# Gated mix of linear attention and a ReLU layer: the first x block evacuated from two banks, all x transposes ahead of the first slab, the gate row behind two later units

## The chip, the cores and the metric

The kernel runs on one core of a Trainium2 chip. The metric is the device time of one execution, in microseconds (us). A core has five engines with a queue each: TensorE (PE: matmuls; its weight loads are listed apart as PEld), VectorE (DVE), ScalarE (ACT), GpSimd (POOL) and SyncE (SP), which here issues nearly all DMA transfers. They run side by side and wait for one another by semaphores. Matmuls write to PSUM, an accumulator of 128 partitions with 8 banks of 512 fp32 columns; VectorE and ScalarE carry results from there to SBUF ("evacuation").

## The reference

```python
x = A_x                                             # [1, 2048, 512] bf16
g = sigmoid((x * gate_w).sum(-1, keepdims=True))    # one gate per row
a = A(x, wqkv, w_phi, wo)                           # linear attention, 32 heads of 16
b = relu(x @ w1) @ w2                               # w1 [512, 1376], w2 [1376, 512]
out = g * a + (1 - g) * b
# A: q, k, v = heads of x @ wqkv;  pq = q @ w_phi, pk = k @ w_phi (per head)
#    phi = concat(softmax(p), softmax(-p));  kv = phi_k^T v,  z = sum phi_k
#    a = concat_heads(phi_q @ kv / (phi_q . z + 1e-6)) @ wo
```

The branch b uses the same x as a. What the change touches is the start of the first matmul of b, x @ w1, and the gate's product x · gate_w.

## The kernel before

**How the work is written.** `_Plan` (L14) holds one list of instructions per engine, in the order in which the Python code calls `p.op` and `p.dma`. Each engine runs its list in that order. An instruction names the events that it waits for (`after`) and the one that it sets (`ev`); events become semaphore counts. There is no scheduler: the order is the one written out. `free[bank]` is a table that is kept while the lists are written: the event after which a PSUM bank may be written again, set by whoever plans the last evacuation of that bank.

**Transposed x.** Matmuls need x with d on the partitions, as XT (4 d tiles of 128, 2048 rows). Rows 0 to 511 (the first "chunk" of four) come as they are, by two loads of 256 rows each (`loadx0`, halves 0 and 1, j = 0, 1 and 2, 3), and are transposed on TensorE by 16 matmuls of 128 columns against the identity IDN (`xtr`, L235), evacuated to XT by VectorE or ScalarE (`xev`, L247). The three other chunks are transposed by DMA (L189) and come much later.

**The start on TensorE**, in its order (L537 to L562): five warm-up matmuls of ones, 512 columns each; the gate row (`gatecol(3)`, L223: the four 128-blocks of gate_w, loaded to GR, are turned by one matmul with 4 output columns in bank 3, and VectorE copies them into column DFF of W1); a sixth warm-up of 384 columns; then the transposes. Called a and b by half, they are: a0 (half 0, d tiles 0 and 1: four blocks, bank 6), the first two blocks of a1 (half 0, d tiles 2 and 3, bank 7), which are all from the first load; then b0 (half 1, d tile 0: two blocks, bank 2), the rest of a1, b1 (half 1, d tiles 1 and 2: four blocks, bank 1). VectorE evacuates a0 in two instructions, ScalarE b0, a1 and b1, in this order. Two transposes are left, b2 (half 1, d tile 3), which use bank 2 again after b0.

**Slabs.** The first eight of the ten units of 128 columns of x @ w1 are not computed unit by unit but by d tile: `slab(t)` (L529) issues, for each of eight units, the matmul of d tile t into the unit's own bank, so that the first slab needs only the first piece of W1. The order of banks is UB = (3, 4, 5, 0, 6, 7, 2, 1). The first slab is cut: four units, then the transposes b2, evacuated by VectorE, then four units; the seventh unit writes bank 2, and so waits for b2's evacuation. `XA` and `XB` name the evacuations that the four slabs wait for. VectorE sets a few tiles to constants (L553 to L560), and eight ReLUs (`relu`, L264) evacuate the units to HT, ScalarE and VectorE in turn.

**Units and banks.** All later units are made by `hunit` (L279: four accumulating matmuls of 512 columns, then a ReLU). They and `rest` (L289, the last 96 columns of w1 with the gate column beside them, for a chunk) and V tile 1 take their bank from `nextbank()` (L275), a counter that gives 3, 4, 5 in turn. Units 8 and 9 of chunk 0 follow the slabs, then V tiles 0 and 1, the products of w_phi and wqkv (`pre`), V tile 2 and `rest(0)`, which is the first to read the gate column.

**The two phases.** The main loop (L586) goes over 16 row tiles: q and k scores (`atile`, banks 0 and 1), V (`vtile`, bank 2), the accumulation of kv (`kv`, banks 6 and 7), and in between units of chunks 1 to 3 by the lists `mid` and `late` (the last six: (3, 4) to (3, 9)). The second phase (L614 to L638) is the output: `nd(m)` (L464: attention output of a row tile, banks 0 and 1 or 2 and 3 by turns), `finB` (L489: relu(x @ w1) @ w2, 11 matmuls), `finA` (L500: attention @ wo) and `comb` (L512: mixes the two and stores). Its banks are written out by hand: `finB(0, 4)` at L617, and (4, 5, 7) in turn for later tiles. All of them wait for `free[bank]`. It begins with

```python
nd(0)
qchain(NT - 1)
gate()
finB(0, 4)
nd(1)
```

With the counter as it stands, the last three units (3, 7), (3, 8), (3, 9) have banks 4, 5 and 3.

Of the kernel before, what the change touches and what calls it, by code (L numbers as in the profile page):

```python
# [5 lines left out]
ACT = mybir.ActivationFunctionType  # L6
# [62 lines left out]
def bass_gated_mix__linear_kernel_hedgehog__dense_activation_relu__prompt_kernel(  # L69
# [17 lines left out]
    P = 128  # L87
# [17 lines left out]
    with ExitStack() as es:  # L105
        E = es.enter_context
        XT = E(nc.sbuf_tensor("XT", [P, NDT, S], BF16))
# [18 lines left out]
        IDN = E(nc.sbuf_tensor("IDN", [P, P], BF16))  # L126
# [14 lines left out]
        PS = E(nc.psum_tensor("PS", [P, 8, 512], FP32))  # L141

        XS = OT[:, 0, :].rearrange("p (j d) -> p j d", j=4)
# [7 lines left out]
        p = _Plan(["sp", "pool", "act", "dve", "pe"])  # L151
        free = {b: [] for b in range(8)}
# [24 lines left out]
        for t in range(1, NDT):  # L177
            loadw1(t, 0, 8 * P)
        p.dma("sp", lambda e: e.dma_start(
            out=W1[:, :, 8 * P:DFF], in_=B_w1[:, 8 * P:DFF].rearrange("(j p) n -> p j n", p=P)), "w1r", ev="w1r")  # L180
        p.dma("sp", lambda e: e.dma_start(
            out=WPS[:, :, :], in_=A_w_phi.rearrange("(g hl) r c -> (hl r) g c", g=NDT)), "wps", ev="wps")
        p.dma("sp", lambda e: e.dma_start(
            out=WV[:, :, :], in_=A_wqkv[:, 2 * D:3 * D].rearrange("(j p) n -> p j n", p=P)), "wv", ev="wv")
        for i in range(2):
            p.dma("sp", lambda e, i=i: e.dma_start_transpose(
                out=WQKT[:, 4 * i:4 * i + 4, :], in_=A_wqkv[:, i * D:(i + 1) * D]), f"wqk{i}", ev=f"wqk{i}")
        for c in range(1, NCH):
            p.dma("sp", lambda e, c=c: e.dma_start_transpose(  # L189
                out=XT[:, :, c * 512:(c + 1) * 512], in_=x2[c * 512:(c + 1) * 512, :]), f"x{c}", ev=f"x{c}")  # L190
# [9 lines left out]
            after=["wps"], ev="wd")  # L200
        for gt in range(NDT):
# [4 lines left out]
                after=["wd", "m8"], ev=f"wbd{gt}")  # L206
# [5 lines left out]
             after=["iota0"], ev="idn")  # L212
        p.op("dve", lambda e: e.tensor_single_scalar(ROW8[:, :], ROW8[:, :], 4, ALU.arith_shift_right),
             after=["iota"], ev="r8")
# [3 lines left out]
             after=["r64"], ev="m32")  # L218

        def xready(c):  # L220
            return ["xa0", "xa1", "xa2", "xb0", "xb1", "xb3"] if c == 0 else [f"x{c}"]

        def gatecol(bank):  # L223
            gp = PS[:, bank, 0:NDT]
            p.op("pe", lambda e: e.matmul(gp, GR[:, :], IDN[:, 0:NDT], start=True, stop=True),  # L225
                 after=["gr", "idn"], ev="gp")
            p.op("dve", lambda e: e.tensor_copy(W1[:, :, DFF:DFF + 1], gp.unsqueeze(2)), after=["gp"], ev="gw")
            free[bank] = ["gw"]

        def warm(n, cols=512):  # L230
            for _ in range(n):
                p.op("pe", lambda e: e.matmul(PS[:, 4, 0:cols], ones[:, 0:P], ones[:, 0:cols], start=True, stop=True),  # L232
                     after=["one"])

        def xtr(nm, h, dts, bank, evacs, part=None):  # L235
            n = 2 * len(dts)
            for i in (range(n) if part is None else part):
                dt, j = dts[i // 2], 2 * h + i % 2
                p.op("pe", lambda e, i=i, dt=dt, j=j: e.matmul(  # L239
                    PS[:, bank, i * P:(i + 1) * P], XS[:, j, dt * P:(dt + 1) * P], IDN[:, :],  # L240
                    start=True, stop=True),
                    after=["idn", f"x0{h}"] + (free[bank] if i == 0 else []), ev=(f"xt{nm}" if i == n - 1 else None))
            if part is not None and n - 1 not in part:
                return []
            return xev(nm, h, dts, bank, n, evacs)

        def xev(nm, h, dts, bank, n, evacs):  # L247
            src = PS[:, bank, 0:n * P].rearrange("p (t c) -> p t c", c=256)
            out = []
            for eng, i0, i1, ev in evacs:  # L250
                d = XT[:, dts[i0]:dts[i0] + i1 - i0, h * 256:(h + 1) * 256]
                s = src[:, i0:i1, :]
                if eng == "dve":
                    out.append(lambda d=d, s=s, ev=ev: p.op(
                        "dve", lambda e: e.tensor_copy(d, s), after=[f"xt{nm}"], ev=ev))  # L255
                else:
                    out.append(lambda d=d, s=s, ev=ev: p.op(
                        "act", lambda e: e.activation(d, s, ACT.Copy), after=[f"xt{nm}"], ev=ev))
            free[bank] = [evacs[-1][3]]
            return out  # L260

        w1all = ["w10a", "w1r"] + [f"w1{t}" for t in range(NDT)]

        def relu(c, kt, bank, eng):  # L264
            dst, src = HT[:, kt, c * 512:(c + 1) * 512], PS[:, bank, :]
            ev = f"rl{c}_{kt}"
            if eng == "act":
                p.op("act", lambda e: e.activation(dst, src, ACT.Relu), after=[f"h{c}_{kt}"], ev=ev)  # L268
            else:
                p.op("dve", lambda e: e.tensor_single_scalar(dst, src, 0.0, ALU.max), after=[f"h{c}_{kt}"], ev=ev)  # L270
            free[bank] = [ev]
# [3 lines left out]
        def nextbank():  # L275
            rot[0] += 1
            return 3 + (rot[0] - 1) % 3

        def hunit(c, kt, eng="act", bank=None):  # L279
            bank = nextbank() if bank is None else bank  # L280
            for t in range(NDT):
                p.op("pe", lambda e, t=t: e.matmul(  # L282
                    PS[:, bank, :], W1[:, t, kt * P:(kt + 1) * P], XT[:, t, c * 512:(c + 1) * 512],
                    start=(t == 0), stop=(t == NDT - 1)),
                    after=(xready(c) + w1all + free[bank] if t == 0 else ()),
                    ev=(f"h{c}_{kt}" if t == NDT - 1 else None))
            relu(c, kt, bank, eng)
# [41 lines left out]
        def atile(m):  # L329
            b = m % NB  # L330
            first = xready(m // 4)
            order = [(dt, w) for dt in range(NDT) for w in range(2)]
            if m - 1 in split:
# [77 lines left out]
        def vtile(m, eng="act", bank=2):  # L411
            b = m % VB
            for dt in range(NDT):
                p.op("pe", lambda e, dt=dt: e.matmul(  # L414
                    PS[:, bank, :], XT[:, dt, m * P:(m + 1) * P], WV[:, dt, :],
                    start=(dt == 0), stop=(dt == NDT - 1)),
                    after=((xready(m // 4) + ["wv"] + free[bank]) if dt == 0 else ()),
                    ev=(f"v{m}" if dt == NDT - 1 else None))
            dst, src = VS[:, b, :, 0:64], PS[:, bank, :].rearrange("p (g c) -> p g c", g=NG)
            after = [f"v{m}"] + ([f"kv{m - VB}"] if m >= VB else [])  # L420
            if eng == "dve":
                p.op("dve", lambda e: e.tensor_copy(dst, src), after=after, ev=f"cv{m}")
            else:
                p.op("act", lambda e: e.activation(dst, src, ACT.Copy), after=after, ev=f"cv{m}")  # L424
            free[bank] = [f"cv{m}"]
# [97 lines left out]


        UB = (3, 4, 5, 0, 6, 7, 2, 1)
        XA = ("xa0", "xa1", "xa2", "xa2")
        XB = ("xb0", "xb1", "xb1", "xb3")

        def slab(t, us=range(8)):  # L529
            for u in us:  # L530
                p.op("pe", lambda e, u=u: e.matmul(  # L531
                    PS[:, UB[u], :], W1[:, t, u * P:(u + 1) * P], XT[:, t, 0:512],
                    start=(t == 0), stop=(t == NDT - 1)),
                    after=["w10a" if t == 0 and u < 4 else f"w1{t}", XA[t], XB[t]] + free[UB[u]],
                    ev=(f"h0_{u}" if t == NDT - 1 else None))

        warm(5)  # L537
        p.early("pe")
        gatecol(3)
        warm(1, 384)  # L540
        ea = xtr("a0", 0, (0, 1), 6, (("dve", 0, 1, "xa0"), ("dve", 1, 2, "xa1")))
        c1 = ("a1", 0, (2, 3), 7, (("act", 0, 2, "xa2"),))
        xtr(*c1, part=(0, 1))
        eb = xtr("b0", 1, (0,), 2, (("act", 0, 1, "xb0"),))
        ec = xtr(*c1, part=(2, 3))
        ed = xtr("b1", 1, (1, 2), 1, (("act", 0, 2, "xb1"),))
        for fn in (ea[0], eb[0], ea[1], ec[0], ed[0]):
            fn()
        slab(0, range(4))
        for fn in xtr("b2", 1, (3,), 2, (("dve", 0, 1, "xb3"),)):  # L550
            fn()
        slab(0, range(4, 8))
        for b in range(VB):  # L553
            p.op("dve", lambda e, b=b: e.memset(VS[:, b, :, 64:65], 1.0), ev=f"one{b}")
        for b in range(2):
# [5 lines left out]
        for t in range(1, NDT):  # L561
            slab(t)  # L562
        for u in range(8):
            relu(0, u, UB[u], ("act", "dve")[u % 2])
        hunit(0, 8)
        hunit(0, 9, "dve")
        vtile(0, "dve")
        vtile(1, "act", nextbank())
        for i in range(4):
# [16 lines left out]
        for m in range(NT):  # L586
# [7 lines left out]
            if m == 3:  # L594
                for a, b in ((0, 4), (4, 7), (7, KU)):
                    p.dma("sp", lambda e, a=a, b=b: e.dma_start(
                        out=W2[:, a:b, :], in_=B_w2[a * P:b * P, :].rearrange("(j p) n -> p j n", p=P)),
                        "w2", ev=f"w2{a}")
                p.dma("sp", lambda e: e.dma_start(out=W2[0:NR, KU, :], in_=B_w2[KU * P:DFF, :]), "w2", ev="w2")
            if m == 5:  # L600
                for a in range(0, NDT, 2):
                    p.dma("sp", lambda e, a=a: e.dma_start(
                        out=WO[:, a:a + 2, :], in_=A_wo[a * P:(a + 2) * P, :].rearrange("(j p) n -> p j n", p=P)),
# [70 lines left out]
```

The softmax here doesn't subtract the row's maximum and nothing guards it: scores larger than these inputs give would overflow.

## Time and profile before

| what | value |
|---|---|
| median of 5 runs | 147.49 us (147.0 to 147.74) |
| the profiled execution's own time | 147.49 us |
| its span (first to last instruction) | 146.2 us |
| TensorE busy | 143.7 us, 98% of the span, 978 matmuls |
| VectorE, ScalarE, GpSimd busy | 92.2, 72.8, 52.2 us |
| TensorE busy in 0 to 2, 2 to 4, 4 to 6, 6 to 8 us | 1.62, 2.00, 2.00, 1.91 us |
| x @ w1 in slabs (L531) | 32 matmuls, 379 ns the median |
| transposes of x (L239) | 16 matmuls |

A line of groups or of the timeline gives the engine (PE, PEld, DVE, ACT), the line in the code, the operation, and "out<-in" with the program's names; "[0.27 <-PE PS L282]" is the idle time of the engine before it and what released it. Matmuls are pipelined: a duration of 379 ns for 512 columns includes the way through the array, and the next one starts 0.216 us later. What one costs is therefore read from start to start.

### The profile page before, as it was taken

To read this page: it belongs to the slowest core of one execution; us is meant where nothing else is said; L and a number is where in the kernel's file an instruction comes from. 1 tells how busy PE (TensorE), PEld (TensorE's weight loads), DVE (VectorE), ACT (ScalarE), POOL (GpSimd) and SP (SyncE) were. 2 spreads that over 40 slices of the span, in tenths; PEclk is the share of its full clock that TensorE was granted. 3 is DMA by queue.
4 is the path that set the end of the run, shared out by engine and by line. 5 is a ranking of instruction groups with operands and counts; after the bars stand their busy time and mean duration, and the time that the engine had idled before them with its cause. 6 is when DMAs were issued, how large, how long until landed. Compare 5 with 4: busy or idle time off the path is not lost.

```text
span 146.2 us, 2537 instructions
## 1 busy us (share of the span) xinstructions
PE 143.7 (98%) x978; PEld 73.1 (50%) x978; DVE 92.2 (63%) x157; ACT 72.8 (50%) x125; POOL 52.2 (36%) x62
## 2 busy tenths in 40 slices
PE   8999999999999999999999999999999999999994
PEld 3444654444545555545555555554444444444443
DVE  3428737777687878678698977664445555555342
ACT  3307467798778778887878862022221111111150
POOL 2031002778868678688869810300000000000000
DMA  6999994023349993335833431354243223222213
GB/s 194 279 259 212 225 173 95 10 62 76 72 78 352 141 218 72 72 72 108 72 78 79 100 72 35 77 108 120 64 103 76 72 72 75 73 72 74 72 45 105
DMA packets 45221, 16.12 MB, mean 110 GB/s; under 512 B 39352, under 2 KB 44568, under 8 KB 45208
## 3 DMA queue, kind: packets, MB, share of 16 engines
q1 hardware_dynamic: 45056, 15.92, 49.5%
q8 instruction: 8, 0.13, 0.4%
q10 hardware_dynamic: 152, 0.03, 0.1%
q14 instruction: 5, 0.04, 0.1%
HBM read 4.41 MB, written 2.10 MB: 44 GB/s over the span
## 4 chain that ended last, share of the span: by engine, by line
PE 98%; DVE 1%; issue 0%; DVEq 0%
PE PS L493 26%; PE PS L282 19%; PE PS L338 18%; PE PS L502 9%; PE PS L414 9%; PE PS L531 5%; PE PS L468 3%; PE PS L436 3%; PE PS L294 2%; PE PS L232 2%; PE PS L239 1%; PE PS L316 1%; DVE WQK L516 1%; DVE XT L255 0%; PE PS L225 0%
## 5 line engine op out<-in xcount | busy, mean ns | idle before, releaser
L493 PE MATMUL PS<-W,HT 128*128 128x512 bf16 (+4 forms) x187 | 40.6, 366 | 0.0
L382 POOL TENSOR_TENSOR EB<-EB,SC 128x1024 bf16<-128x1024 bf16 x15 | 28.9, 1930 | 24.1 <-DVE SC L380 24.1
L358 ACT ACTIVATE EB<-PS 128x480 bf16<-128x480 f32 (+1 forms) x44 | 30.1, 756 | 14.2 <-PE PS L338 14.2
L507 ACT ACTIVATE TFA<-PS,GT 128x512 bf16<-128x512 f32 x16 | 11.0, 687 | 42.7 <-PE PS L502 42.7
L282 PE MATMUL PS<-XT,W 128*128 128x512 bf16 x128 | 30.7, 379 | 0.0
L338 PE MATMUL PS<-WQK,XT 128*128 128x480 bf16 x128 | 28.5, 366 | 0.0
L378 DVE TENSOR_REDUCE ZB<-EB 128x64 f32<-128x1024 bf16 x15 | 18.3, 1220 | 14.3 <-ACT EB L358 14.3
L516 DVE SCALAR_TENSOR_TENSOR WQK<-PS,OMG,TFA 128x512 bf16<-128x512 f32 (+2 forms) x17 | 12.2, 718 | 23.6 <-ACT TFA L507 22.4
L493 PEld LDWEIGHTS PS<-W,HT 128*128 128x128 bf16 (+1 forms) x187 | 17.1, 98 | 17.4
L268 ACT ACTIVATE HT<-PS 128x512 bf16<-128x512 f32 x35 | 20.3, 614 | 7.4 <-PE PS L531 5.5
L338 PEld LDWEIGHTS PS<-WQK,XT 128*128 128x128 bf16 x128 | 12.5, 98 | 13.6
L282 PEld LDWEIGHTS PS<-XT,W 128*128 128x128 bf16 x128 | 12.0, 98 | 13.2
L393 DVE TENSOR_REDUCE ZB<-EB 128x64 f32<-128x1024 bf16 x16 | 18.6, 1164 | 0.0
L402 POOL TENSOR_TENSOR EB<-EB,SC 128x512 bf16<-128x512 bf16 x16 | 17.0, 1060 | 1.3
L414 PE MATMUL PS<-WV,XT 128*128 128x512 bf16 x64 | 16.2, 378 | 0.0
L502 PE MATMUL PS<-WO,OT 128*128 128x512 bf16 x64 | 16.1, 378 | 0.0
L478 DVE TENSOR_TENSOR WQK<-PS,RDEN 128x512 bf16<-128x512 f32 x16 | 11.1, 691 | 0.5
L502 PEld LDWEIGHTS PS<-WO,OT 128*128 128x128 bf16 x64 | 6.1, 97 | 7.2
L424 ACT ACTIVATE VS<-PS 128x512 bf16<-128x512 f32 x14 | 8.5, 608 | 2.0 <-PE PS L414 2.0
L380 DVE RECIPROCAL SC<-ZB 128x64 f32<-128x64 f32 x16 | 8.8, 553 | 0.5
L414 PEld LDWEIGHTS PS<-WV,XT 128*128 128x128 bf16 x64 | 5.5, 97 | 4.9
L468 PEld LDWEIGHTS PS<-KVNZ,PHQ 128*128 128x128 bf16 x128 | 6.1, 97 | 3.6
(57 smaller groups left out, 88.8 us busy)
## 6 DMA issues: line engine op xcount, KB each, us to landing
out_dram<-WQK SPq DMA_DIRECT2D x15, 128.0 KB, 1.7
W<-in_B_w_dram SPq DMA_DIRECT2D x3, 256.0 KB, 5.0
W<-in_B_w_dram SPq DMA_DIRECT2D x2, 384.0 KB, 5.5
OT<-in_A_x_dram SPq DMA_DIRECT2D x2, 256.0 KB, 3.0
WV<-in_A_wqkv_dram SPq DMA_DIRECT2D x1, 512.0 KB, 6.5
W<-in_B_w_dram SPq DMA_DIRECT2D x1, 512.0 KB, 4.4
WO<-in_A_wo_dram SPq DMA_DIRECT2D x2, 256.0 KB, 3.4
W<-in_B_w_dram SPq DMA_DIRECT2D x1, 352.0 KB, 6.0
```

The costliest lines, as they stand in the source:

```text
L268: p.op("act", lambda e: e.activation(dst, src, ACT.Relu), after=[f"h{c}_{kt}"], ev=ev)
L282: p.op("pe", lambda e, t=t: e.matmul(PS[:, bank, :], W1[:, t, kt * P:(kt + 1) * P], XT[:, t, c * 512:(c + 1) * 512], start=(t == 0), stop= ...
L338: p.op("pe", lambda e, dt=dt, which=which: e.matmul(PS[:, which, 0:DE], XT[:, dt, m * P:(m + 1) * P], WQK[:, which, dt * DE:(dt + 1) * DE] ...
L358: p.op("act", lambda e: e.activation(dst, s_, ACT.Exp, scale=scale), after=[f"qk{m}"] + busy, ev=ev)
L378: p.op("dve", lambda e: e.tensor_reduce(zk, ek, AX.X, ALU.add), after=[emk, f"cst{b}"], ev=f"zk{m}")
L382: p.op("pool" if m < NT - 1 else "dve", lambda e: e.tensor_tensor(EB[:, b, 3, :].rearrange("p (g f) -> p g f", f=DH), EB[:, b, 2, :].rearr ...
L393: p.op("dve", lambda e: e.tensor_reduce(ZB[:, b, 0:64].rearrange("p (h s) -> p h s", s=2), bass.AP(tensor=EB, offset=base, ap=[[EBS, P], [ ...
L402: p.op("pool", lambda e: e.tensor_tensor(EB[:, b, 0, :].rearrange("p (h s f) -> p h s f", h=H, s=2)[:, :, 1, :], EB[:, b, 1, :].rearrange( ...
L414: p.op("pe", lambda e, dt=dt: e.matmul(PS[:, bank, :], XT[:, dt, m * P:(m + 1) * P], WV[:, dt, :], start=(dt == 0), stop=(dt == NDT - 1)), ...
L493: p.op("pe", lambda e, kt=kt, M=M: e.matmul(PS[:, bank, 0:n], HT[0:M, kt, m * P:(m + 1) * P], W2[0:M, kt, cs], start=(kt == 0), stop=(kt = ...
L502: p.op("pe", lambda e, t=t: e.matmul(PS[:, bank, :], OT[:, t, m * P:(m + 1) * P], WO[:, t, :], start=(t == 0), stop=(t == NDT - 1)), after ...
L516: p.op("dve", lambda e: e.scalar_tensor_tensor(out=OSB[:, ob, cs], in0=PS[:, bank, 0:n], scalar=OMG[:, m:m + 1], in1=TFA[:, m % 2, cs], op ...
```

## The change

The transposes are called by block now. `xtr(nm, js, dts, bank)` issues the blocks of the row groups `js` (A = j 0, 1; B = j 2, 3) and d tiles `dts`; `xev` plans one evacuation of a bank by one engine. What differs in what the engines do:

- Half 1 of d tile 0 was b0, two blocks in bank 2, evacuated by ScalarE in one instruction of 256 columns. It is now c0 (j = 2, bank 2, ScalarE, 128 columns) and d0 (j = 3, bank 0, VectorE, 128 columns).
- Half 0 of d tiles 0 and 1 were a0, four blocks in bank 6 evacuated in two VectorE instructions that waited for the fourth block. They are now a0 (bank 6) and a1 (bank 5), and a0's evacuation waits for its own two blocks.
- Half 1 of d tile 3, which stood in the middle of the first slab, is now b3 in bank 6, and all 16 transposes come ahead of the slab. The first slab is no longer cut.
- VectorE's order is a0, d0, a1, b3; ScalarE's is c0, a2, b1.
- The gate row's matmul leaves the start. It comes after units 8 and 9, ahead of V tile 0, in a bank from `nextbank()`, and waits for that bank. Its copy on VectorE comes after the ReLU of unit 9.
- `nextbank()` is called once more, so V tile 1, `rest(0)` and all later units have the next bank of the three. The last three units have banks 5, 3 and 4. The banks of the second phase are as before.

```diff
         def xready(c):
-            return ["xa0", "xa1", "xa2", "xb0", "xb1", "xb3"] if c == 0 else [f"x{c}"]
+            return [f"xv{n}" for n in ("a0", "a1", "a2", "c0", "d0", "b1", "b3")] if c == 0 else [f"x{c}"]
...
             p.op("pe", lambda e: e.matmul(gp, GR[:, :], IDN[:, 0:NDT], start=True, stop=True),
-                 after=["gr", "idn"], ev="gp")
+                 after=["gr", "idn"] + free[bank], ev="gp")
...
+        def xtr(nm, js, dts, bank, last=True, off=0):
+            blocks = [(dt, j) for dt in dts for j in js]
+            for i, (dt, j) in enumerate(blocks):
+                o = off + i * P
+                p.op("pe", lambda e, dt=dt, j=j, o=o: e.matmul(
+                    PS[:, bank, o:o + P], XS[:, j, dt * P:(dt + 1) * P], IDN[:, :], start=True, stop=True),
+                    after=["idn", f"x0{j // 2}"] + (free[bank] if o == 0 else []),
+                    ev=(f"xt{nm}" if last and i == len(blocks) - 1 else None))
+
+        def xev(eng, nm, js, dts, bank):
+            w = len(js) * P
+            d = XT[:, dts[0]:dts[-1] + 1, js[0] * P:js[0] * P + w]
+            s = PS[:, bank, 0:len(dts) * w].rearrange("p (t c) -> p t c", c=w)
...
+            free[bank] = [f"xv{nm}"]
...
-        XA = ("xa0", "xa1", "xa2", "xa2")
-        XB = ("xb0", "xb1", "xb1", "xb3")
-
-        def slab(t, us=range(8)):
-            for u in us:
+        XV = (("xva0", "xvc0", "xvd0"), ("xva1", "xvb1"), ("xva2", "xvb1"), ("xva2", "xvb3"))
+
+        def slab(t):
+            for u in range(8):
...
-                    after=["w10a" if t == 0 and u < 4 else f"w1{t}", XA[t], XB[t]] + free[UB[u]],
+                    after=["w10a" if t == 0 and u < 4 else f"w1{t}", *XV[t]] + (free[UB[u]] if t == 0 else []),
...
+        A, B = (0, 1), (2, 3)
         warm(5)
         p.early("pe")
-        gatecol(3)
         warm(1, 384)
-        ea = xtr("a0", 0, (0, 1), 6, (("dve", 0, 1, "xa0"), ("dve", 1, 2, "xa1")))
-        c1 = ("a1", 0, (2, 3), 7, (("act", 0, 2, "xa2"),))
-        xtr(*c1, part=(0, 1))
-        eb = xtr("b0", 1, (0,), 2, (("act", 0, 1, "xb0"),))
-        ec = xtr(*c1, part=(2, 3))
-        ed = xtr("b1", 1, (1, 2), 1, (("act", 0, 2, "xb1"),))
-        for fn in (ea[0], eb[0], ea[1], ec[0], ed[0]):
-            fn()
-        slab(0, range(4))
-        for fn in xtr("b2", 1, (3,), 2, (("dve", 0, 1, "xb3"),)):
-            fn()
-        slab(0, range(4, 8))
+        xtr("a0", A, (0,), 6)
+        xtr("a1", A, (1,), 5)
+        xtr("a2", A, (2,), 7, last=False)
+        xtr("c0", (2,), (0,), 2)
+        xtr("d0", (3,), (0,), 0)
+        xtr("a2", A, (3,), 7, off=2 * P)
+        xev("dve", "a0", A, (0,), 6)
+        xev("act", "c0", (2,), (0,), 2)
+        xev("dve", "d0", (3,), (0,), 0)
+        xev("act", "a2", A, (2, 3), 7)
+        xev("dve", "a1", A, (1,), 5)
+        xtr("b1", B, (1, 2), 1)
+        xtr("b3", B, (3,), 6)
+        xev("act", "b1", B, (1, 2), 1)
+        xev("dve", "b3", B, (3,), 6)
+        slab(0)
...
         hunit(0, 9, "dve")
+        gatecol(nextbank())
         vtile(0, "dve")
```

More of the change, by code (lines that the diff above doesn't have):

```diff
@@ L233, in warm @@
                      after=["one"])
[L235 to L260, printed above, removed]
+        def xtr(nm, js, dts, bank, last=True, off=0):
[6 more added lines that the diff above has]
+                    ev=(f"xt{nm}" if last and i == len(blocks) - 1 else None))
@@ new lines, in xev @@
+        def xev(eng, nm, js, dts, bank):
+            w = len(js) * P
+            d = XT[:, dts[0]:dts[-1] + 1, js[0] * P:js[0] * P + w]
+            s = PS[:, bank, 0:len(dts) * w].rearrange("p (t c) -> p t c", c=w)
+            if eng == "dve":
+                p.op("dve", lambda e: e.tensor_copy(d, s), after=[f"xt{nm}"], ev=f"xv{nm}")
+            else:
+                p.op("act", lambda e: e.activation(d, s, ACT.Copy), after=[f"xt{nm}"], ev=f"xv{nm}")
+            free[bank] = [f"xv{nm}"]
```

## The prediction

> **What bounds the kernel now.** I read the page first: the span, the busy shares and the chain that ended last.
>
> ```profile
> span 146.2 us, 2537 instructions
> PE 143.7 (98%) x978; PEld 73.1 (50%) x978; DVE 92.2 (63%) x157; ACT 72.8 (50%) x125; POOL 52.2 (36%) x62
> PE 98%; DVE 1%; issue 0%; DVEq 0%
> ```
>
> TensorE is the kernel: 98% of the chain is its own work. So only two things can move the end: time in which TensorE stands still, and time in which it runs slowly. Next I asked for the waits of its weight loads (PEld waits where PE does) over the whole span, to see where it stands still; each row is the total, the count and the longest.
>
> ```profile
> PEld PS L531 <- DVE VS L554: 0.6, 1, 0.6
> PEld PS L239 <- DMA OT<-in_A_x_dram: 0.4, 2, 0.2
> ```
>
> After about 7 us no row is left: from there to the end TensorE never waits. The first row is named after a memset (L554), but its place is the chain between 2 and 8 us, in order of time (start, length, what):
>
> ```profile
> 3.15 1.59 PE PS L239 x14
> 4.73 1.32 PE PS L531 x4
> 6.06 0.13 PE PS L239 x2
> 6.18 0.02 issue
> 6.21 0.42 DVE XT L255
> 6.63 0.05 DVE VS L554 x2
> 6.68 0.00 issue
> 6.69 1.47 PE PS L531 x6
> ```
>
> The chain leaves TensorE once: for the evacuation of the last two transposes (L255, 0.42). The seventh unit of the first slab writes to bank 2, in which they lie, so it starts at 6.69. Narrow windows of the timeline give the starts of single matmuls: the sixth unit at 6.22, which streams 0.216, so TensorE is empty from 6.43 to 6.69, 0.25 us. A second hole lies in front of the slab (timeline from 4.4 to 4.7):
>
> ```profile
> 4.10 0.63 PE L239 MATMUL PS<-IDN,OT 128*128 128x128 bf16 x4
> 4.13 0.87 ACT L258 ACTIVATE XT<-PS 128x256 bf16<-128x256 f32 x2 [1.73 <-PE PS L239]
> 4.66 0.58 PE L531 MATMUL PS<-XT,W 128*128 128x512 bf16 x1
> ```
>
> The last of the 14 transposes starts at 4.42 and they are 0.107 apart, so TensorE is free at 4.52; the slab needs both halves of d tile 0, and ScalarE's evacuation of the second half runs from 4.13 to 4.51 (0.384). The slab starts at 4.66: a hole of 0.13. Last, the place where the second phase begins, from 87.3 to 91.2:
>
> ```profile
> 88.09 0.42 PE L468 MATMUL PS<-KVNZ,PHQ 128*128 128x68 bf16 x8
> 88.29 0.60 ACT L268 ACTIVATE HT<-PS 128x512 bf16<-128x512 f32 x1 [0.27 <-PE PS L282]
> 88.34 2.54 PE L493 MATMUL PS<-W,HT 128*128 128x512 bf16 x11
> ```
>
> The ReLU here is that of the last unit, (3, 9). It runs while TensorE is already in finB(0): in the kernel before they use different banks (3 and 4).
>
> **What the Trainium skill says.** "TensorE: Matmul & The Clock Gate", Part 1: the array starts at half rate and gets its full rate after a window of about 3.4 us of activity that runs freely and isn't tied to the kernel's start. The trace agrees: the second slab unit takes 0.42 from start to start (5.03 to 5.46), the third 0.216. So in this execution the full rate came at about 5.45; it may come elsewhere in another. "PSUM — Partial Sum Buffer", PSUM bank collisions raise a hardware error: two engines must not be in one bank at once; hence two engines need two banks for one block, and finB must wait for a ReLU in its bank. "Perfetto Trace Analysis", Optimizing Tensor Performance: independent groups should rotate through banks so that evacuation overlaps the next group; the trace shows just that (ReLU at 88.29 beside finB at 88.34).
>
> **The change part by part.** All sums are made against the profiled execution: 147.49 us, of which 146.2 is the span; it equals the median of the runs, 147.49.
>
> *Transposes and first slab.* The order of the first six transposes and the waits for the two x loads stay (they land at about 2.88 and 3.65), so they run from 2.94 and the next ten from 3.70. Ten at half rate: 3.70, 3.78, then 0.107 each; the last starts at 4.63 and TensorE is free at 4.74. Is the slab's data there by then? A transpose that signals is followed by its evacuation 0.352 later (the first: 3.26 to 3.61). The third block of d tile 0 (c0) signals at 3.70, so ScalarE starts at 4.05; 128 columns aren't in the trace, but 256 take 0.384 and 512 about 0.597, so about 0.28: ready at 4.33. The fourth (d0) signals at 3.78, VectorE starts at 4.13 (its first job, a0, is now released after two transposes instead of four and is over at about 3.82); 256 columns take 0.423 and 512 0.69, so 128 take about 0.29: ready at 4.42. If a 128-column evacuation cost as much as one of 256, they would be ready at 4.43 and 4.55, and both are before 4.74 still. The slab starts at 4.74 with no hole, not at 4.66. First unit 4.74 to 5.17 at half rate; the second, two thirds through at 5.45, ends at about 5.52; six at 0.216: the second slab starts at 6.82. Before it started at 7.13. **Gain 0.31.** The two late transposes cost 0.11 before at full rate, and 0.21 now at half rate; that is in the sum.
>
> Does something else come late? Unit 3 (bank 5) needs a1, third in VectorE's order, over at about 4.82, used at 5.52. Unit 5 (bank 6) needs b3, signalled at 4.63, evacuated from about 4.98 to 5.41, used at 5.95. Unit 8 needs b1 on ScalarE, behind c0 and a2: about 5.46, used at 6.6. The W1 pieces for slabs 2, 3 and 4 land at 6.13, 7.41 and 8.12, used at 6.82, 8.5 and 10.3; wqkv's first transpose lands at 13.63, used at about 15.4. VectorE's memsets move forward with b3, by about 1.2 us. What follows keeps its order, so the gain is carried on: TensorE has no wait there to lose it in.
>
> *Gate row.* Its matmul (4 columns) took 0.05 from its start to the next before, in front of transposes that waited for x anyway; now it sits between units and V tile 0 and costs that 0.05 (bounds: 0.03, the spacing of the 68-column matmuls at L468, and 0.1). Its copy on VectorE (0.18) falls into the gap between unit 9's ReLU (ends 14.93) and the copy of V tile 0 (starts 15.10); without that gap it would delay that copy by 0.18, whose bank is wanted only 0.8 us after the copy's end. The transposes don't start sooner without it: they wait for x. **Loss 0.05.** No DMA moves in SP's, ScalarE's or POOL's order.
>
> *The bank counter.* `gatecol(nextbank())` takes one more bank from the rotation of 3, 4, 5, so every later unit is one bank further. In between this changes nothing, since a bank still comes round after three takes. At the end it does. Before, the last three units use 4, 5, 3; now 5, 3, 4. finB(0, 4) names bank 4 in full, and so now waits for the ReLU of the last unit, which ended at 88.29 + 0.60 = 88.89. nd(0) alone (0.26) lies between. From the end of an evacuation to the released matmul took 0.06 where the weight load itself waits (6.63 to 6.68) and 0.14 where a separate wait stands ahead of it (4.51 to 4.66). finB(0) would start at 88.95 to 89.03 instead of 88.34. **Loss 0.60 to 0.69, I take 0.64**: finB's first matmul has several waits. Behind it in TensorE's queue stands all the rest of the kernel, which had no hole in which to take it back; nd(1), which waited for this ReLU before, finds it done.
>
> Sum: −0.31 + 0.05 + 0.64 = +0.38, so 147.49 + 0.38 = **147.87 us**, +0.26%. About 0.3% (0.44 us) is what a measurement of this kernel can tell from no change, so this counts as no change, hard by the line.
>
> **The rivals.**
>
> *Slower: the gain at the start doesn't come, the stall does.* The mechanism is the clock: if the full rate comes before the transposes are over, at about 3.8, TensorE is done with them sooner, and the slab waits for d0 on VectorE until about 4.56; and if slab unit 5 then waits for b3, the gain shrinks. It is decided by whether the evacuations stay ahead of TensorE: from a delay of 0.3 us on in a0, d0, a1, b3 the gain is gone. For it: VectorE now has a0, d0, a1, b3 in one line. Against it: every need above has 0.3 us or more in hand. Price: 0.05 + 0.64 = +0.69, 148.18 us (+0.47%).
>
> *Faster: the stall at the end isn't there.* For it: what stands behind nd(0) in TensorE's queue might be pulled ahead of the wait. Against it: in this trace only weight loads start ahead of a running matmul, and here it is finB's first weight load that has to wait. Or the ReLU could be earlier: no, it is released by its own matmul (0.27 idle before it). Price: −0.31 + 0.05 = −0.26, 147.23 us (−0.18%); with a clock that comes early, before's hole at bank 2 grows and the gain may reach 0.5: 147.0, and that is the only way to more than 0.3% faster.
>
> *It doesn't do what it says:* if d0 or b1 turned out to bind the slab, one hole would take the place of another: gain 0.1, 148.1 us.
>
> **How the numbers follow.** The sum as worked out: 0.66, at 147.87 with its own range of 147.65 to 148.1, of which two fifths lie beyond +0.44. No gain or little of it, stall in full: 0.22, at about 148.15, four fifths beyond the line. No stall: 0.12, at 147.0 to 147.25, half of it beyond −0.3%. Slower: 0.66 × 0.4 + 0.22 × 0.8 = 0.44; faster 0.06; within 0.3% 0.50. The range from 147.25 to 148.25 leaves out about a tenth below and a tenth above. The runs before spread from 147.0 to 147.74 themselves.
>
> **What would show it.** In the changed kernel's timeline: the 16 transposes in one run, the slab's first matmul at about 4.74, eight slab matmuls with no gap, the second slab at about 6.8; no wait of a weight load for VectorE near 6.7. The gate's matmul after unit 9. A wait of finB(0)'s first weight load for ScalarE's ReLU of about 0.6 us, near 88, right behind the first eight matmuls on KVNZ, and TensorE dense on either side. The prediction is wrong if that wait is missing or lasts under 0.4, if the second slab starts after 7.0, or if a new wait of TensorE appears between 13 and 20 us, where the gate row was put.

## The result and the profile after

The changed kernel takes 147.68 us (median of 43 runs, 147.2 to 148.36), beside 147.25 us for the kernel before (median of 80 runs, 146.82 to 148.27). The ratio is 1.0025, with a 95% interval of 1.0016 to 1.0035: slower by a quarter of a percent, within the 0.3% and clear of zero. The prediction was +0.26% (147.87 us, counted from the 147.49 us of the five runs that it had). The profiled execution of the changed kernel took 147.67 us, its span is 146.4 us.

Page of the changed kernel: the span, the busy shares and the engines of the chain that ended last.

```profile
span 146.4 us, 2538 instructions
PE 143.5 (98%) x978; PEld 73.5 (50%) x978; DVE 92.5 (63%) x158; ACT 72.8 (50%) x125; POOL 52.2 (36%) x62
PE 97%; DVE 1%; ACT 0%; issue 0%; DVEq 0%
```

Nearly the same picture, except that ScalarE stands in the chain now. Its chain between 2 and 8 us (start, length, what) answers the eight lines shown of before:

```profile
1.84 1.17 PE PS L232 x3
3.02 1.71 PE PS L239 x16
4.73 3.30 PE PS L522 x14
```

The chain doesn't leave TensorE any more: 16 transposes in one run, the slab right behind them (L522 is L531 of before). Both holes are gone, that ahead of the slab and that ahead of the seventh unit. The chain between 86 and 91 us has a new one:

```profile
85.99 1.74 PE PS L274 x8
87.73 0.02 issue
87.76 0.61 ACT HT L260
88.36 0.14 issue
88.50 2.54 PE PS L485 x11
```

It goes from the last unit's matmuls (L274) over its ReLU on ScalarE (L260) to finB(0) (L485), past nd(0). The timeline from 87.3 to 91.2 shows why:

```profile
87.56 0.42 PE L460 MATMUL PS<-KVNZ,PHQ 128*128 128x68 bf16 x8
87.76 0.60 ACT L260 ACTIVATE HT<-PS 128x512 bf16<-128x512 f32 x1 [0.27 <-PE PS L274]
88.47 2.07 PEld L485 LDWEIGHTS PS<-W,HT 128*128 128x128 bf16 x11 [0.62 <-issue]
88.50 2.54 PE L485 MATMUL PS<-W,HT 128*128 128x512 bf16 x11 [0.53 <-ACT HT L260]
```

Before, the matmul of finB(0) started 0.05 after the start of the ReLU; now it starts 0.14 after its end. The last of the eight matmuls on KVNZ starts at 87.78, and with 0.03 for itself finB(0) could have followed at 87.81: the hole is 0.69 us.

**The clock has to be taken out before two profiles are compared.** TensorE's full rate came at different times in the profiles. In the changed kernel the second slab unit starts at 4.95 and the third at 5.28 (two narrow windows of the timeline, at 5.4 and at 5.5; each shows two units):

```profile
4.95 0.71 PE L522 MATMUL PS<-XT,W 128*128 128x512 bf16 x2
5.28 0.59 PE L522 MATMUL PS<-XT,W 128*128 128x512 bf16 x2
```

From start to start a unit takes 0.427 us at half rate (the one before these, 4.52 to 4.95) and 0.216 at full rate (those behind). The 0.330 us lie between: 0.23 at half rate and the rest at full rate, so the rate changed at 5.18. In the same way, before gives 5.46. A microsecond at half rate does the work of half a microsecond. Where TensorE has work all the time, a full rate that comes later by some time therefore delays the rest by half of that time, and I take half of the difference to 5.46 off the times that come after it:

| kernel | second x load landed | full rate from | second slab | corrected | last matmul starts | corrected |
|---|---|---|---|---|---|---|
| before | 3.65 | 5.46 | 7.13 | 7.13 | 144.00 | 144.00 |
| changed | 3.44 | 5.18 | 6.58 | 6.71 | 144.16 | 144.29 |
| e1, banks 4 and 5 exchanged | 3.37 | 6.20 | 7.12 | 6.75 | 144.01 | 143.64 |
| e3, gate row in bank 6 | 3.55 | 6.15 | 7.11 | 6.77 | 144.01 | 143.66 |
| e4, gate row at the start | 3.62 | 6.30 | 7.24 | 6.82 | 144.11 | 143.69 |
| e5, old evacuations | 3.63 | 5.41 | 6.79 | 6.81 | 143.68 | 143.70 |
| e7, one more VectorE instruction | 3.56 | 5.59 | 6.84 | 6.77 | 143.73 | 143.67 |

So the start gained 7.13 − 6.71 = 0.42 us, and the end lost 144.29 − 144.00 = 0.29 us all the same. The difference, some 0.7, lies between: the hole of 0.69 and 0.03 for the gate row. e2, e6 and e8 got their full rate before the slab or in its first unit (3.58, 4.73, 4.30), where a faster TensorE partly just waits longer; they are left out of the table for that.

### The profile page after: what moved, and what is told of

It is laid out like the page before. It is cut to its first block, busy times and chain, and to the rows that moved or that the text cites. A ratio compares the mean times of both kernels' runs of the same rounds, so it can differ in the third digit from the quotient of the medians.

```text
span 146.4 us, 2538 instructions
## 1 busy us (share of the span) xinstructions
PE 143.5 (98%) x978; PEld 73.5 (50%) x978; DVE 92.5 (63%) x158; ACT 72.8 (50%) x125; POOL 52.2 (36%) x62
## 4 chain that ended last, share of the span: by engine, by line
PE 97%; DVE 1%; ACT 0%; issue 0%; DVEq 0%
PE PS L485 26%; PE PS L274 19%; PE PS L330 18%; PE PS L494 9%; PE PS L406 9%; PE PS L522 5%; PE PS L428 3%; PE PS L460 3%; PE PS L286 2%; PE PS L232 2%; PE PS L239 1%; PE PS L308 1%; DVE WQK L508 1%; ACT HT L260 0%; DVE ONE L208 0%
## 5 line engine op out<-in xcount | busy, mean ns | idle before, releaser
L485 PE MATMUL PS<-W,HT 128*128 128x512 bf16 (+4 forms) x187 | 40.6, 366 | 0.5 <-ACT HT L260 0.5
L274 PE MATMUL PS<-XT,W 128*128 128x512 bf16 x128 | 30.7, 379 | 0.0
L485 PEld LDWEIGHTS PS<-W,HT 128*128 128x128 bf16 (+1 forms) x187 | 17.0, 98 | 18.0 <-issue 0.6
L260 ACT ACTIVATE HT<-PS 128x512 bf16<-128x512 f32 x35 | 20.3, 614 | 7.1 <-PE PS L522 5.2
L274 PEld LDWEIGHTS PS<-XT,W 128*128 128x128 bf16 x128 | 12.0, 98 | 13.2
L466 DVE RECIPROCAL RDEN<-PS 128x32 f32<-128x32 f32 x16 | 5.6, 350 | 3.8 <-PE PS L460 3.8
```

Source lines behind the costliest of these rows:

```text
L274: p.op("pe", lambda e, t=t: e.matmul(PS[:, bank, :], W1[:, t, kt * P:(kt + 1) * P], XT[:, t, c * 512:(c + 1) * 512], start=(t == 0), stop= ...
L485: p.op("pe", lambda e, kt=kt, M=M: e.matmul(PS[:, bank, 0:n], HT[0:M, kt, m * P:(m + 1) * P], W2[0:M, kt, cs], start=(kt == 0), stop=(kt = ...
```

## The experiments

Theory: the start gains, and the whole of the loss is finB(0) waiting for the last unit's ReLU, because the gate row takes a bank of the rotation. Rivals: the loss comes from the gate row itself, from the new order at the start, or from any user of a bank. All ratios are to the kernel before, measured on the same chip.

### Banks 4 and 5 exchanged in the second phase

```diff
-        finB(0, 4)
+        finB(0, 5)
-        FB = (4, 5, 7)
+        FB = (5, 4, 7)
-            finB(m, (4, 3)[i], cs, "ab"[i])
+            finB(m, (5, 3)[i], cs, "ab"[i])
```

> The changed kernel with banks 4 and 5 exchanged in the whole second phase: finB(0, 5), later tiles (5, 4, 7), the last tile (5, 3). The rotation keeps its extra take, the gate row stays behind unit 9. Theory (the stall is finB(0) waiting for the ReLU of the last unit because both have bank 4): finB(0) now follows a ReLU two units back, the hole of 0.69 us behind the first eight matmuls on KVNZ is gone, and the kernel is faster than before by the gain at the start alone: 0.26 us (ratio 0.998) to 0.5 us (0.9966). Rival (the hole only moves to the next user of a bank, or has another cause): time like the changed kernel, +0.37 us, ratio 1.0025.

Measured: 146.9 us, ratio 0.998 (0.9965 to 0.9996). Timeline of this kernel from 87.2 to 89:

```profile
88.10 0.42 PE L460 MATMUL PS<-KVNZ,PHQ 128*128 128x68 bf16 x8
88.30 0.60 ACT L260 ACTIVATE HT<-PS 128x512 bf16<-128x512 f32 x1 [0.27 <-PE PS L274]
88.35 0.81 PE L485 MATMUL PS<-W,HT 128*128 128x512 bf16 x3
```

finB(0) runs beside the ReLU again, as before. The gate row still takes its bank of the rotation and stands where the change put it: so neither is a loss by itself; what costs the time is that the last unit and finB(0) have the same bank. No other wait took its place; the only wait of TensorE's weight loads for a transfer was at the start, for W1's first piece, which landed at 4.58 here:

```profile
PEld PS L522 <- DMA W<-in_B_w_dram: 0.2, 1, 0.2
```

### Before, with one bank skipped

```diff
         hunit(0, 9, "dve")
+        nextbank()
```

> The kernel before with one bank of the rotation skipped after unit 9 and nothing else: no gate row there, start as before. Theory: the whole stall and nothing of the gain, +0.65 to +0.69 us, ratio 1.0044 to 1.0047, and one hole of about 0.69 us in TensorE ahead of finB(0). Rival (the skipped bank is harmless, the loss comes from the gate row or from the order at the start): ratio 1.000, no hole.

Measured: 147.98 us (6 runs), ratio 1.0068 (1.0045 to 1.0092). Its waits, and its timeline from 87.3 to 89:

```profile
PEld PS L493 <- issue: 0.6, 1, 0.6
```

```profile
87.58 0.42 PE L468 MATMUL PS<-KVNZ,PHQ 128*128 128x68 bf16 x8
87.78 0.60 ACT L268 ACTIVATE HT<-PS 128x512 bf16<-128x512 f32 x1 [0.27 <-PE PS L282]
88.52 0.81 PE L493 MATMUL PS<-W,HT 128*128 128x512 bf16 x3 [0.53 <-ACT HT L268]
```

One line that computes nothing makes the hole, at the same size to the nanosecond (0.688 beyond the spacing of the matmuls, as in the changed kernel). The time lost is 0.66 to 1.35 us by the interval; the trace gives 0.69, at its lower end. (The ratio itself lies above the expected 1.0044 to 1.0047; six runs don't tell whether that is chance.) The rival that blames the gate row or the order at the start falls.

### The gate row in bank 6

```diff
-        gatecol(nextbank())
+        gatecol(6)
```

> The changed kernel with the gate row in bank 6 in place of one from the rotation; the gate row stays behind unit 9. Theory: as with the exchanged banks, no hole ahead of finB(0), ratio 0.9966 to 0.998 (0.26 to 0.5 us faster than before). Rival (the gate row itself, its wait or its copy on VectorE costs some tenths where it now stands): ratio 1.000 or more, and a wait of TensorE between 13 and 20 us.

Measured: 147.14 us, ratio 0.999 (0.9974 to 1.0006), just beyond the expected values. The interval takes in a part of them and also the rival's 1.000, so the times don't decide; the trace does. It has no hole ahead of finB(0), and corrected for the clock its last matmul starts at 143.66, within 0.06 of all others without the hole; this profile's clock came 0.7 us later than that of before. There is no wait of TensorE between 13 and 20 us. In the changed kernel the gate row's place looks like this (timeline from 13.4 to 14.6):

```profile
13.48 0.17 PE L225 MATMUL PS<-IDN,GR 128*128 128x4 bf16 x1
13.51 1.45 PE L406 MATMUL PS<-WV,XT 128*128 128x512 bf16 x6
14.29 0.16 DVE L227 CAST W<-PS 128x4 bf16<-128x4 f32 x1
14.57 0.69 DVE L414 CAST VS<-PS 128x512 bf16<-128x512 f32 x1
```

From its start to that of the next matmul it is 0.03 us, and VectorE's copy ends at 14.46, ahead of the V tile's copy at 14.57.

### The gate row at the start

```diff
         p.early("pe")
+        gatecol(3)
         warm(1, 384)
...
         hunit(0, 9, "dve")
-        gatecol(nextbank())
```

> The changed kernel with the gate row back in its old place at the start (bank 3, between the warm-ups), so the rotation is as before. It has the new transposes and evacuations alone. Theory as predicted (the transposes wait for x anyway, so the gate row at the start costs nothing): as with bank 6, or up to 0.05 us faster, ratio 0.9963 to 0.998. Rival (where x lands early the gate row, which waits for its own load, holds up the transposes): slower than with bank 6 by 0.1 to 0.17 us, ratio 0.998 to 0.9993, and in the trace the first transpose starts right behind the sixth warm-up and not at x's landing.

Measured: 146.83 us, ratio 0.998 (0.9958 to 1.0001). The times don't tell it from bank 6 (0.999). The traces tell a part: this kernel from 2.5 to 3.2, and the changed one from 2.4 to 3.0:

```profile
2.71 0.19 PE L225 MATMUL PS<-IDN,GR 128*128 128x4 bf16 x1
2.76 0.48 PE L232 MATMUL PS<-ONE 128*128 128x384 bf16 x1
3.04 0.42 PE L239 MATMUL PS<-IDN,OT 128*128 128x128 bf16 x2
```

```profile
2.82 0.41 PE L239 MATMUL PS<-IDN,OT 128*128 128x128 bf16 x2
```

x's first load landed at 2.73 and 2.68. With the gate row ahead, which waits for its own load (2.67), the first transpose starts at 3.04 instead of 2.82. That is the picture of the rival. But the second x load takes nearly all of it back. Here the transposes end at 4.74, without waiting for that load, which landed at 3.62. In e5, below, the gate row isn't at the start and the second load landed at the same time (3.63); there the transposes wait for it and end at 4.71. What is left is 0.03 us at half rate, some 0.015 us of time, against 0.03 for the gate row's later place. So the gate row's move is worth about nothing either way, but not for the reason that I gave.

### The evacuations of before, all transposes ahead

```diff
-        xtr("a0", A, (0,), 6)
-        xtr("a1", A, (1,), 5)
+        xtr("a0", A, (0, 1), 6)
         xtr("a2", A, (2,), 7, last=False)
-        xtr("c0", (2,), (0,), 2)
-        xtr("d0", (3,), (0,), 0)
+        xtr("c0", B, (0,), 2)
         xtr("a2", A, (3,), 7, off=2 * P)
...
-        xtr("b3", B, (3,), 6)
+        xtr("b3", B, (3,), 0)
+        for i, n in enumerate(("xva0", "xva1")):
+            p.op("dve", lambda e, i=i: e.tensor_copy(
...
+                after=["xta0"], ev=n)
...
-        xev("act", "c0", (2,), (0,), 2)
-        xev("dve", "d0", (3,), (0,), 0)
+        xev("act", "c0", B, (0,), 2)
...
-        xev("dve", "b3", B, (3,), 6)
+        xev("dve", "b3", B, (3,), 0)
```

(with `gatecol(6)`, and without d0 in the two lists of evacuations to wait for.)

> As with the gate row in bank 6, but the evacuations of the kernel before: half 1 of d tile 0 in one bank, one ScalarE instruction of 256 columns; d tiles 0 and 1 of half 0 in one bank, waiting for the fourth block. All 16 transposes stay ahead of the slab, the last two in bank 0. It tells whether the two banks and two engines do anything. Measure: start of the second slab, corrected for where the clock came (half of the time by which the full rate came after 5.46 us is taken off): before 7.13, changed 6.71, bank 6 6.77. Theory as predicted (the transposes hide the evacuations): 6.7 to 6.8, no hole between the last transpose and the first slab matmul, ratio to before 0.997 to 0.999, as with bank 6. Rival (the split carries the gain): a hole of 0.1 to 0.2 us ahead of the slab, 6.9 or more.

Measured: 146.91 us, ratio 0.9973 (0.996 to 0.9987). Chain between 2 and 8 us, and a line of its timeline from 3.9 to 5.2:

```profile
3.65 0.02 issue
3.67 1.25 PE PS L239 x10
4.92 3.11 PE PS L522 x13
```

```profile
4.10 1.36 ACT L251 ACTIVATE XT<-PS 128x256 bf16<-128x256 f32 x3 [1.71 <-PE PS L239]
```

The block evacuated in one piece (ScalarE, the first of the three, 4.10 to 4.49) is ready before the last transpose has streamed (4.71), and the slab follows without a hole. The two banks and two engines, the change's first-named part, gain nothing that can be seen: what they make faster is hidden behind the transposes that now come ahead. In this trace the margin is 0.08 us: 4.49, and the 0.14 that pass from an evacuation's end to the matmul that it releases, against 4.71. So in an execution in which TensorE is faster there the split may still gain something. Over the runs it doesn't show: e7, which has the split, was measured on the same chip and has the same ratio, 0.9973.

### The last two transposes back in the slab

```diff
-        xtr("b3", B, (3,), 6)
...
-        xev("dve", "b3", B, (3,), 6)
-        slab(0)
+        slab(0, range(4))
+        xtr("b3", B, (3,), 2)
+        xev("dve", "b3", B, (3,), 2)
+        slab(0, range(4, 8))
```

(with `gatecol(6)`, and `slab(t, us)` as in the kernel before.)

> As with the gate row in bank 6, but the last two transposes are back in the middle of the first slab, in bank 2, as in the kernel before; evacuations of d tile 0 stay split. It tells what taking them out of the slab is worth. Theory: the hole of 0.25 us ahead of the seventh unit is back, second slab corrected at 6.95 to 7.05 (0.2 to 0.3 later than with bank 6), ratio to before 0.999 to 1.000. Rival (the split at the front carries the gain): 6.75 to 6.85.

Measured: 147.35 us, ratio 1.0005 (0.9992 to 1.0018): the gain is gone. Its waits:

```profile
PEld PS L522 <- DMA W<-in_B_w_dram: 0.6, 1, 0.6
PEld PS L522 <- DVE VS L550: 0.6, 1, 0.6
```

The second row is the hole of before: the sixth unit starts at 5.88, the seventh at 6.34, 0.25 more than its spacing. The first is the piece of W1 for the second slab, which landed at 7.02 in this execution; the clock came early (4.73), and the second slab, which could have started at 6.78, had to wait until 7.07. Corrected, 6.78 is 7.15, more than expected (6.95 to 7.05). The second x load landed 0.21 later than with bank 6, which at half rate puts 0.1 us of time on top. How often that piece of W1 comes so late in the other runs isn't known, so not all of the loss need be the hole's; but with e5, which keeps the two transposes ahead and has the gain in full without the split, the gain at the start is that of taking the two transposes out of the slab. Ahead of the slab there is no hole here: the last of the 14 transposes starts at 4.53 and the first unit at 4.64. So the split does close the hole of 0.13 us of before; at half rate that is some 0.07 us of time, too little for these runs to show.

### One more VectorE instruction ahead of d0

```diff
+        p.op("dve", lambda e: e.memset(SC[:, 0:4, :], 0.0))
         xev("dve", "d0", (3,), (0,), 0)
```

(with `gatecol(6)`.)

> As with the gate row in bank 6, with one more VectorE instruction (a memset of 128 x 512 fp32, some 0.3 to 0.6 us) between the evacuations a0 and d0, so that d0, a1 and b3 come that much later. It tells how much room the new VectorE order has. Theory as predicted (room of about 0.3 us at d0): with x landing as in the runs so far d0 ends at 4.2 to 4.4 without it, and the slab could start 0.14 later; with 0.4 more it starts at about 4.8 to 4.95 in place of 4.52 to 4.64, a hole of 0.2 to 0.3 at half rate, second slab corrected 0.1 to 0.25 later, 6.85 to 7.0; ratio 0.999 to 1.0005. Rival (VectorE has room to spare): as with bank 6.

Measured: 146.96 us, ratio 0.9973 (0.9959 to 0.9987): no loss. Timeline from 3.7 to 4.7:

```profile
3.83 0.48 DVE L540 MEMSET SC<- 128x512 f32 x1
4.23 0.55 DVE L249 CAST XT<-PS 128x128 bf16<-128x128 f32 x2
4.60 0.20 PEld L522 LDWEIGHTS PS<-XT,W 128*128 128x128 bf16 x2
4.64 0.63 PE L522 MATMUL PS<-XT,W 128*128 128x512 bf16 x1
```

The memset took 0.48, but about half of it in the time in which VectorE waited for d0's transpose anyway. d0 ended at 4.46, against 4.32 with bank 6: a delay of 0.14, not of 0.4. The first matmul of the slab started at 4.64, just where the last transpose had streamed, as it would have without the memset; the second slab starts at 6.77, corrected, as with bank 6. (That matmul's weight load, at 4.60, came 0.04 after the landing of W1's first piece at 4.55, so d0 wasn't what it waited for; in e1 that landing and the weight load are 4.58 and 4.62.) So the expectation failed on the size of the dose: a delay of 0.14 at d0 costs nothing, and the edge wasn't reached. Where it lies can be estimated from bank 6's trace. With the 0.14 that a release took in the kernel before, 4.32 makes 4.46, 0.18 ahead of 4.64; with the 0.10 of e6, where d0 ended at 4.54 and the slab's first matmul started at 4.64, it is 0.22.

### nd(1) ahead of finB(0)

```diff
         nd(0)
+        nd(1)
         qchain(NT - 1)
         gate()
         finB(0, 4)
-        nd(1)
```

> The changed kernel with nd(1) pulled ahead of finB(0): the rotation and the banks stay, and eight matmuls on KVNZ (0.26 us) more stand between the last unit and the matmul that waits for its ReLU. Theory (the hole is the end of that ReLU plus some 0.14, less the end of what stands ahead of finB(0)): the hole shrinks by just these 0.26 us, from 0.69 to 0.43, and the kernel with it: ratio to before 1.0025 - 0.0018 = 1.0007. Rival (the hole is a fixed cost, or nd(1) gets a wait of its own because its VectorE work now stands ahead of the last row tile's chain): hole still 0.6 or more or a second hole near 91 us, ratio 1.002 or more.

Measured: 147.37 us, ratio 1.000 (0.998 to 1.002), too wide to tell 1.0007 from the rival's 1.002; the trace tells. Timeline from 87.2 to 89:

```profile
87.29 0.67 PE L460 MATMUL PS<-KVNZ,PHQ 128*128 128x68 bf16 x16
87.49 0.60 ACT L260 ACTIVATE HT<-PS 128x512 bf16<-128x512 f32 x1 [0.27 <-PE PS L274]
88.23 1.02 PE L485 MATMUL PS<-W,HT 128*128 128x512 bf16 x4 [0.27 <-ACT HT L260]
```

Sixteen small matmuls fill what eight did, and the hole shrinks from 0.69 to 0.43 us, by the 0.26 that was put in. The wait still ends 0.14 after the ReLU's end, and TensorE's weight loads have no other wait behind the start. The hole is an end that is fixed by ScalarE, less the work that stands ahead of it.

## Why the prediction was right

*The sum.* Predicted −0.31 + 0.05 + 0.64 = +0.38 us; the traces, corrected for the clock, give −0.42 + 0.03 + 0.69 = +0.30, and their ends differ by 0.29; the ratio of the runs is +0.37 us (0.0025 × 147.25). Each term has the right sign and place, and each was off by 0.02 to 0.11. That +0.37 meets +0.38 to a hundredth is luck: the interval of the ratio goes from 0.24 to 0.52 us, and the errors of the terms partly cancel. None of the three signs of being wrong came up: the wait lasts 0.62 us in the weight loads, the second slab starts at 6.58, and TensorE has no wait between 13 and 20 us.

*The stall at the end* was the step that decided, and it came where it was put. I took 0.64 between 0.60 and 0.69; it was the upper value, since a separate wait stands ahead of finB's first weight load, as in the case of 4.51 to 4.66. That it comes from the shared bank is shown from three sides: e2 makes it with nothing else, e1 and e3 take it away and leave the new start and the gate row's later place, and e8 shortens it by what is put ahead of it. The program waits so that two engines don't use one bank at once; what happens without that wait was not run.

*The gain at the start* was 0.42 instead of 0.31. In the changed kernel's profile the second x load landed 0.21 earlier than in that of before, and at half rate 0.21 is 0.11 of time: the whole difference. Where it landed as before (3.63 in e5 and 3.62 in e4), the second slab starts at 6.81 and 6.82, corrected; the prediction was 6.82. The holes ahead of the slab and ahead of the seventh unit are gone. The prediction gave the 0.31 to the new start as a whole; e5 and e6 show that the two transposes carry it. The durations estimated for 128 columns were 0.28 and 0.29; the trace has 0.278 (ScalarE) and 0.291 (VectorE).

*The gate row* cost 0.03, the lower bound. The reason given for the old place costing nothing, that the transposes wait for x anyway, is wrong where x lands early: e4 has the first transpose held up by 0.22. It held only because the second load binds next.

*The room at d0* was put at 0.3 us or more. From d0's end to the slab it is that (4.32 to 4.64 with bank 6), but the 0.10 to 0.14 from an evacuation's end to the released matmul was left out, so some 0.2 is usable; e7 used 0.14 of it without loss. The list of what could come late also left out W1's first piece, which the slab's first unit needs: it held the slab up in e1 and e8.

*The rivals.* That the stall isn't there fell with the first trace. That the gain doesn't come when the clock is early was not seen, but e8, with the same start and the full rate from about 4.30, comes near it (its timeline from 4.4 to 4.7):

```profile
4.18 0.50 PE L239 MATMUL PS<-IDN,OT 128*128 128x128 bf16 x5
4.57 0.11 PEld L522 LDWEIGHTS PS<-XT,W 128*128 128x128 bf16 x2
4.58 0.39 PE L522 MATMUL PS<-XT,W 128*128 128x512 bf16 x1
```

The last transpose starts at 4.46 and takes 0.06 at full rate, so TensorE is free at 4.52; the slab starts 0.06 later. What it waited for is W1's first piece, which landed at 4.53. But d0 ended at 4.40, and with 0.10 to 0.14 for the release the slab could have started at 4.50 to 4.54 at the earliest: with a clock this early hardly any room is left at d0. A clock before 3.8 with the new start didn't come up in a profile, so that end stays open. That d0 or b1 binds the slab came up in no trace of the new start.

A kernel that beats both follows from this: the transposes ahead, and the gate row in any bank outside the rotation, or the second phase's banks 4 and 5 exchanged. Measured: 0.9973 (e5, 0.996 to 0.9987), 0.9973 (e7), 0.998 (e1), 0.999 (e3). The traces of these end within 0.06 us of one another once corrected, so I take the four for the same kernel in time, some 0.3 us faster than before; e3's own interval, up to 1.0006, doesn't show it alone.

## What to carry to other kernels

A counter that gives out buffers in turn is part of the schedule of everything behind it: a single extra take at 13 us moved the last unit into the bank that the next phase names by hand, 75 us later. Where a rotation meets names written out by hand, write down which buffer comes last, and keep one-off users out of the rotation. And when several engines' steps are made faster at once, ask which one is still waited for: here moving two transposes gained all that the runs show, and splitting an evacuation nothing that they show.

## What the runs showed of the hardware

TensorE's full rate came at 3.58, 4.30, 4.73, 5.18, 5.41, 5.46, 5.59, 6.15, 6.20 and 6.30 us in the ten profiles, although all kernels begin with the same five warm-up matmuls at 0.38 us. This fits what the Trainium skill says ("TensorE: Matmul & The Clock Gate", Part 1: the activity window isn't tied to the kernel's start). The same part gives ±500 ns for the scatter of that moment from run to run; here 2.7 us lie between the earliest and the latest. The moment makes a time of its own: of the kernels without a hole, those with the full rate at 5.41 and 5.59 start their last matmul at 143.68 and 143.73, those at 6.15 to 6.30 at 144.01 to 144.11, some 0.34 us for 0.72 us. That is as large as the whole effect studied, and would account for much of the spread of 1.45 us between runs of the kernel before; that it is the only cause wasn't tested.

Second, with the transposes out of the way W1's pieces are next: the first landed at 4.58 in e1 and at 4.53 in e8, the one for the second slab at 7.02 in e6, and each of the three held TensorE up.
